# Delta rule and routed experts: batch 1 of expert 0 gets dates of its own in the planner

## The chip, the cores and the metric

The kernel runs on one core of one Trainium2 chip. The metric is the device time of one execution in microseconds. The engines are TensorE (PE; its weight loads are shown apart as PEld), VectorE (DVE), ScalarE (ACT), GpSimd (POOL) and SyncE (SP, which here only issues transfers). The granted clock of PE is given as a share of full speed.

## The reference

The first half is a delta rule over 4 batches x 8 heads, 768 steps, head size 48; its outputs, regrouped, are the 3072 tokens (384 wide) of a router that sends each token to two of eight experts, each two matrices with a ReLU between.

```python
k_n = k / (np.linalg.norm(k, axis=-1, keepdims=True) + 1e-06)
for t in range(S):
    y[:, :, t] = np.einsum('bhd,bhde->bhe', q[:, :, t], state)
    v_old = np.einsum('bhde,bhd->bhe', state, kt)
    state = state + bt[:, :, :, None] * np.einsum('bhd,bhe->bhde', kt, vt - v_old)
...
logits = x @ w_gate
noise_scale = np.log1p(np.exp(x @ w_noise))
noisy_logits = logits + noise_scale * noise
top2 = np.argpartition(-noisy_logits, 2, axis=1)[:, :2]
...
h = np.maximum(x[mask] @ w1[e], 0.0)
out[mask] += top2_w[mask, k, None] * (h @ w2[e])
```

## The kernel before

**The delta rule in chunks.** The 768 steps are 12 chunks of 64. A unit is one chunk of two batches, so there are 24 units, n = 0 to 23, in two independent state streams; four units (two chunks) make a step s = 0 to 5. For each step one triangular matrix per head and chunk is inverted on DVE, column by column (`invert`, lines 743 and 747; the results `tb` and `tt` are written at lines 770 and 778), after which PE joins blocks (`join`, lines 821 and 827). A unit then goes through `within` (the product of queries and keys, masked on DVE into qk, line 864), `recur` (state times keys on PE, line 612; the difference from v on DVE, line 914; state times queries, "of_state", line 885; "solve", line 930; the new state, gathered on PE at line 952 and added on DVE at line 964) and `answer` ("of_chunk", line 989; the store of the rows of y, line 395; the turn of y, line 999; the router product with `wgn`, line 1004, whose result ACT copies to the logits, line 1035). The turns of k and q are at line 594. `v` is multiplied by norms on POOL (line 894).

**Routing.** `route` handles steps 0 and 1, steps 2 and 3, step 4 and step 5, in four turns: ACT and DVE find the two experts and their weights, PE counts earlier tokens of each expert (`count_earlier`, lines 1126 to 1132), DVE makes row numbers, and POOL scatters one list entry per token and choice into `tokens_x` in DRAM by indirect transfers ("spreads", line 437). `cut` caps a count.

**Early tiles.** Expert 0's first five tiles of 128 tokens are worked on as soon as the list holds enough: batch 1 (tiles 0 and 1) after step 1's routing, batch 2 (tiles 2 and 3) after step 3, batch 3 (tile 4) after step 4. For a batch, `early` loads its list (`load_meta`, SP, line 1268), gathers token rows (POOL, line 401), turns them (PE, line 1294; copied by ACT, line 1302), multiplies them in eight groups by `w1` (PE, line 1313; ReLU on ACT, line 1324), back by `w2` (PE, line 1337, in four pieces a tile), scales by the gate (DVE, line 1349), and, for batch 1 alone, adds them to `out` by an indirect transfer at once (`put_early`, POOL, line 456).

**The planner.** None of this is emitted in program order. Every piece above is a job with an engine, an estimated cost, readers and writers, PSUM banks and an optional due time. `Jobs.order` plays the jobs through in time by those estimates and fixes one order for every engine. Among jobs that could start at the same moment it takes the one with the smallest key. Due times are handed back from a job to those before it. Each engine then executes its jobs in exactly that order, whatever the real times are; an instruction that waits holds up everything behind it on its engine. Early jobs carry `late`, which sorts them behind all other jobs:

```python
job.key = (0, job.due) if job.late is None else (1, job.late)
```

**After the rule** (`rest`, and a loop over experts 1 to 7, written out by hand): SP loads the lists of all experts once the last spreads have landed (line 421), POOL gathers the rest of expert 0 and expert 1's rows `xr` (line 401), SP regroups `xr` into `xq` (line 1562), DVE turns that into `xe` (line 1572) and makes sums of its blocks (line 1514). PE finishes the rest of expert 0 (lines 1686 to 1712) and starts expert 1 with the products of the sums (line 1548). Experts 1 to 7 follow each other with PE as the busiest engine. `t_w`, `s_w`, `s_x` are sums of weight and token blocks.

Of the kernel before, what the change touches and what calls it, by code (L numbers as in the profile page):

```python
# [25 lines left out]
EARLY_BANK = 2, (0, 1, 2)  # L26
EARLY = {1: [(0, 2)], 3: [(2, 4)], 4: [(4, 5)]}
EARLY_TILES = 5
PUT_IN_RULE = 1
ROWS = TILES * 128 + MORE  # L30
META = 3
# [65 lines left out]
class Jobs:  # L97
# [13 lines left out]
        self.wrote, self.read = {}, {}  # L111

    def add(self, engine, cost, emit, reads=(), writes=(), opens=None, uses=None, closes=None,
            lands=0.0, moves=0.0, due=None, late=None, apart=0.0):
        job = SimpleNamespace(
            engine=engine, cost=cost * (self.SLOW if engine == self.PE else 1.0), emit=emit, opens=opens, closes=closes, lands=lands,
            moves=moves,
            due=1e9 if due is None else due, late=late, apart=apart, after=set(),
            number=len(self.jobs),
        )  # L120
        bank = opens or uses or closes
        if bank:

            if bank.users:
                job.after.add(bank.users[0])
            if closes:
                job.after.update(bank.users)
            if uses and engine == self.PE:
                job.after.update(bank.users)
            bank.users.append(job.number)  # L130
        for key in reads:
            job.after.update(self.wrote.get(key, ()))
        for key in writes:
            job.after.update(self.wrote.get(key, ()))
            job.after.update(self.read.get(key, ()))
        for key in reads:
            self.read.setdefault(key, []).append(job.number)
        for key in writes:
            self.wrote[key], self.read[key] = [job.number], []
        job.after.discard(job.number)  # L140
        self.jobs.append(job)

    def order(self):
        jobs = self.jobs
        for job in reversed(jobs):
            for i in job.after:
                jobs[i].due = min(jobs[i].due, job.due - job.cost - self.SIGNAL)
        for job in jobs:
            job.key = (0, job.due) if job.late is None else (1, job.late)
        waits = [len(job.after) for job in jobs]  # L150
        then = [[] for _ in jobs]
        for job in jobs:
            for i in job.after:
                then[i].append(job.number)
        ready = [0.0] * len(jobs)
        could = [set() for _ in self.ENGINES]
        for job in jobs:
            if not job.after:
                could[job.engine].add(job.number)
        free = [0.0] * len(self.ENGINES)  # L160
        empty = {size: [0.0] * len(x) for size, x in self.banks.items()}
        spaced = moved = 0.0

        def place(size, among):

            return min(
                ((empty[size][i], i) for i in among if empty[size][i] is not None),
                default=None,
            )

        done = []
        while len(done) < len(jobs):
            first = {}
            best = None
            for engine in self.ENGINES:
                at = []
                for i in could[engine]:
                    start = max(free[engine], ready[i], spaced if jobs[i].apart else 0.0)
                    if jobs[i].opens:
                        which = jobs[i].opens.size, jobs[i].opens.among  # L180
                        if which not in first:
                            first[which] = place(*which)
                        room = first[which]
                        if room is None:
                            continue
                        start = max(start, room[0])
                    at.append((start, jobs[i].key, i))
                if at:
                    soon = min(at)[0] + self.PATIENCE
                    pick = min((x for x in at if x[0] <= soon), key=lambda x: x[1:])  # L190
                    best = min(best or (1e9,), pick)
            start, _, i = best
            job = jobs[i]
            could[job.engine].remove(i)
            end = free[job.engine] = start + job.cost
            if job.apart:
                spaced = start + job.apart
            if job.opens:
                size, among = job.opens.size, job.opens.among
                job.opens.at = x = first[size, among][1]  # L200
                empty[size][x] = None
                job.opens.tile = self.banks[size][x]
                for y in job.opens.users:
                    if jobs[y].late is None:
                        jobs[y].key = 0, min(jobs[y].due, end + self.SOON)
            if job.closes:
                empty[job.closes.size][job.closes.at] = end + self.SIGNAL
            job.start = start
            if job.moves:
                end = moved = max(moved, end) + job.moves  # L210
            done.append(job)
            for j in then[i]:
                ready[j] = max(
                    ready[j],
                    end + (self.SIGNAL + job.lands if jobs[j].engine != job.engine else 0.0),
                )
                waits[j] -= 1
                if not waits[j]:
                    could[jobs[j].engine].add(j)
        return sorted(done, key=lambda job: job.start)  # L220
# [13 lines left out]
def kernel(  # L234
# [52 lines left out]
    FT = F // 128  # L287
# [178 lines left out]
    def deltanet(ictx):  # L466
# [4 lines left out]
        jobs = Jobs(  # L471
            [psum.tile([128, 512], FP32, name=f"single{i}") for i in range(2)],
            [psum.tile([128, 2, 512], FP32, name=f"pair{i}") for i in range(3)],
        )
        PE, ACT, DVE, POOL, SP = Jobs.ENGINES
# [771 lines left out]
        early_xe = sb([128, KT, 256], "early_xe")  # L1247
        early_hT = sb([128, FT, 256], "early_hT")
# [7 lines left out]
        def early(s, lo, hi):  # L1256
# [2 lines left out]


            n, rows = hi - lo, (hi - lo) * 128
            w1e, w2e = held["w"]
            of_steps = [
                ("rows", x, i, y) for x in range(s + 1) for i in range(US) for y in (0, 1)
# [2 lines left out]
            def load_meta():  # L1267
# [7 lines left out]

            jobs.add(
                SP, 0.7, load_meta, reads=of_steps, writes=[("early_meta", lo)], lands=2.0,
                moves=0.3, late=lo,
            )
            units = (s + 1) * US  # L1280
            for i in range(n):
                at = lo + i
                x, x_key = early_x[at % 4], ("early_x", at % 4)
                jobs.add(
                    POOL, 1.2,
                    lambda x=x, at=at: [take_rows(x, place_of(early_meta[:, at]), units)],
                    reads=[("early_meta", lo), *(("stored", i) for i in range(units))],
                    writes=[x_key], lands=2.0, moves=0.7, late=lo,
                )
                p = early_bank()  # L1290

                def turned_rows(x=x, p=p):
                    for do in range(KT):
                        nc.tensor.transpose(
                            flat(p)[:, do * 128 : (do + 1) * 128],
                            chunk(x, do), ident,
                        )

                jobs.add(PE, 0.5, turned_rows, reads=[x_key], opens=p, late=lo)
                jobs.add(  # L1300
                    ACT, 0.5,
                    lambda i=i, p=p: nc.scalar.copy(
                        early_xe[:, :, i * 128 : (i + 1) * 128],
                        flat(p)[:, 0 : KT * 128].rearrange("p (k t) -> p k t", t=128),
                    ),
                    writes=[("early_xe", i)], closes=p, late=lo,
                )
            for fo in range(FT):
                p = early_bank()

                def inner_of(fo=fo, p=p):
# [5 lines left out]

                jobs.add(
                    PE, 0.0038 * rows, inner_of, reads=[("early_xe", i) for i in range(n)] + ["w1"],
                    late=lo + 0.1, opens=p,  # L1320
                )
                jobs.add(
                    ACT, 0.12 + rows * 0.0011,
                    lambda fo=fo, p=p: nc.scalar.activation(
                        early_hT[:, fo, 0:rows], flat(p)[:, 0:rows], ACTF.Relu
                    ),
                    writes=[("early_hT", fo)], closes=p, late=lo + 0.1,
                )
            for i in range(n):
                at = lo + i  # L1330
# [2 lines left out]
                for f0 in range(0, FT, 2):  # L1333

                    def back(i=i, p=p, f0=f0):
# [4 lines left out]
                            )  # L1340

                    jobs.add(
                        PE, 0.98, back, late=lo + 0.2,
                        reads=[("early_hT", f0), ("early_hT", f0 + 1), "w2"],
                        **({"uses": p} if f0 else {"opens": p}),
                    )
# [3 lines left out]
                        got, flat(p)[:, 0:DM], early_meta[:, at, 1:2]  # L1350
                    ),
                    reads=[("early_meta", lo)], writes=[got_key], closes=p, late=lo + 0.2,
                )
                if s > PUT_IN_RULE:
                    held["puts"].append(lambda got=got, at=at: put_early(got, at))
# [525 lines left out]
```

## Time and profile before

| | |
|---|---|
| median of 3 runs | 817.26 us (814.52 to 818.99) |
| profiled execution | 819.58 us, of which the span from first to last instruction is 817.8 us |
| granted PE clock, mean of the span | 0.897 |
| busy PE, DVE, POOL, ACT | 727.6, 566.7, 414.3, 311.6 us |
| last router product of the rule ends | 325.3 us |
| expert 1 begins on PE | 395.5 us |

PE is busy 89% of the span, but the span has stages with different limits. Expert 1 and what follows take about half of it. The other half is the delta rule, and between the two stands a stretch in which PE works on early tiles and the rest of expert 0 while POOL, SP and DVE bring up expert 1's tokens. Where a row of the timeline has brackets, they give the idle time of the engine just before the row and what ended it.

### The profile page before, as it was taken

What the parts mean: (1) busy time and instruction counts of PE and PEld (TensorE: products, weight loads), DVE (VectorE), ACT (ScalarE), POOL (GpSimd) and SP (SyncE); (2) the same over time, 40 slices, a digit from 0 to 9 for tenths busy, and PEclk for the clock granted to TensorE, in tenths of its full rate; (3) what the DMA queues carried; (4) which work ended last, traced back from release to release, by engine and by line L of the source; (5) the groups of instructions that cost most, each with busy time, mean ns of one, the idle gap of its engine ahead of it and who ended that gap; (6) DMA issues with size and microseconds to landing.
All of it is one profiled execution on the core that took longest, in us unless ns stands there. A gap on an engine that the chain in (4) does not pass through costs nothing.

```text
span 817.8 us, 22648 instructions
## 1 busy us (share of the span) xinstructions
PE 727.6 (89%) x9365; PEld 572.8 (70%) x9365; DVE 566.7 (69%) x1256; ACT 311.6 (38%) x740; POOL 414.3 (51%) x398
## 2 busy tenths in 40 slices
PE   4665887887889889999999999999999999999993
PEld 3445776676778779778568678578587597596693
DVE  4899889998899631303588487587686785785841
ACT  3547394846764542112250430430521511502500
POOL 2102100105520633569677786886886886787032
PEclk9955789768868656999999999999999999999998
DMA  2465636633333102464645444553445346333031
GB/s 47 78 111 126 184 96 157 175 73 67 61 72 71 43 23 40 156 105 84 183 112 120 126 132 83 146 154 56 144 142 104 100 138 129 89 59 43 0 38 26
DMA packets 142928, 79.61 MB, mean 97 GB/s; under 512 B 118624, under 2 KB 139232, under 8 KB 141792
## 3 DMA queue, kind: packets, MB, share of 16 engines
q1 hardware_dynamic: 128096, 57.94, 27.1%
q0 software_dynamic: 12544, 19.75, 13.7%
q8 instruction: 75, 1.23, 0.7%
q10 hardware_dynamic: 2176, 0.39, 0.3%
q14 instruction: 37, 0.30, 0.2%
HBM read 49.85 MB, written 20.03 MB: 85 GB/s over the span
## 4 chain that ended last, share of the span: by engine, by line
PE 60%; DVE 21%; issue 10%; POOL 3%; SPq 2%; ACT 1%; DMA 0%; DVEq 0%; POOLq 0%; ACTq 0%
PE inner L1548 25%; PE outer L1548 14%; DVE part L743 6%; DVE t L747 5%; PE pair L1313 3%; PE pair L1337 3%; PE pair L612 2%; POOL out_dram L456 2%; PE inner L1659 2%; PE single L1004 1%; SPq L546 1%; DVE t L662 1%; DVE qk L864 1%; PE pair L989 1%; SPq L562 1%
## 5 line engine op out<-in xcount | busy, mean ns | idle before, releaser
L1615 ACT ACTIVATE hT<-inner 128x416 f32<-128x416 f32 x112 | 57.9, 517 | 260.8 <-PE inner L1548 259.4
L1609 DVE TENSOR_TENSOR hT<-hT,inner 128x416 f32<-128x416 f32 x182 | 105.6, 587 | 64.0 <-PE inner L1548 55.9
L456 POOL DMA_INDIRECT out_dram<-sums,metas_x x51 | 83.6, 1639 | 94.4 <-DVE sums L1448 67.1
L437 POOL DMA_INDIRECT tokens_x<-meta,slot x48 | 48.7, 1014 | 97.8 <-DVE t L756 33.0
L1548 PE MATMUL inner<-s_x,w1e 128*128 128x416 f32 x196 | 78.7, 512 | 0.0
L743 DVE TENSOR_TENSOR part<-t 128x30 f32<-128x30 f32 (+9 forms) x180 | 69.2, 384 | 4.7
L747 DVE TENSOR_TENSOR t<-t,part 128x30 f32<-128x30 f32 (+9 forms) x180 | 64.3, 357 | 6.2
L1604 ACT ACTIVATE hT<-hT 128x416 f32<-128x416 f32 x112 | 59.9, 547 | 12.1 <-DVE hT L1609 6.8
L401 POOL DMA_INDIRECT xr<-rows_y,metas_x x49 | 56.4, 1152 | 14.0 <-issue 13.0
L712 POOL TENSOR_SCALAR_AFFINE_SELECT t<-t 128x1024 f32<-128x1024 f32 x6 | 7.6, 1268 | 107.5 <-DVE ss L683 107.5
L1548 PEld LDWEIGHTS inner<-s_x,w1e 128*128 128x128 f32 x196 | 37.2, 190 | 31.2 <-issue 29.0
L1548 PE MATMUL inner<-xe,w1e 128*128 128x416 f32 x140 | 58.1, 513 | 0.0
L1548 PE MATMUL outer<-t_w,hT 128*128 128x192 f32 x336 | 58.0, 326 | 0.0
L1548 PE MATMUL inner<-s_x,s_w 128*128 128x416 f32 x140 | 56.9, 512 | 0.0
L1548 PEld LDWEIGHTS outer<-t_w,hT 128*128 128x128 f32 x336 | 55.2, 190 | 0.0
L1514 POOL TENSOR_TENSOR w1e<-w1e 128x256 f32<-128x256 f32 x63 | 53.5, 858 | 2.3
L1548 PE MATMUL outer<-w2e,hT 128*128 128x192 f32 x280 | 50.7, 328 | 0.3
L1548 PEld LDWEIGHTS outer<-w2e,hT 128*128 128x128 f32 x280 | 46.1, 190 | 4.3 <-issue 2.2
L894 POOL TENSOR_TENSOR v<-v,norms 128x384 f32<-128x384 f32 x24 | 22.8, 967 | 46.3 <-DVE norms L726 25.5
L1548 PEld LDWEIGHTS inner<-s_x,s_w 128*128 128x128 f32 x140 | 26.6, 190 | 22.3 <-issue 22.3
L1548 PEld LDWEIGHTS inner<-xe,w1e 128*128 128x128 f32 x140 | 26.4, 190 | 20.7 <-issue 16.2
L801 ACT COPY w<-tt 32x256 f32<-32x256 f32 x96 | 38.6, 402 | 5.5 <-DVE tt L778 3.5
(191 smaller groups left out, 1594.1 us busy)
## 6 DMA issues: line engine op xcount, KB each, us to landing
w1e<-in_moe_w_dram SPq DMA_DIRECT2D x8, 1536.0 KB
w2e<-in_moe_w_dram SPq DMA_DIRECT2D x8, 1536.0 KB
xq<-xr SPq DMA_DIRECT2D x56, 84.0 KB
qp<-in_q_dram SPq DMA_DIRECT2D x48, 96.0 KB
v<-in_v_dram SPq DMA_DIRECT2D x48, 96.0 KB
out_dram<-empty SPq DMA_DIRECT2D x4, 1152.0 KB
rows_y<-y SPq DMA_DIRECT2D x24, 192.0 KB
kp<-in_k_dram SPq DMA_DIRECT2D x88, 48.0 KB
```

The lines of the kernel that those rows point to most:

```text
L401: d = nc.gpsimd.indirect_dma_start(out=got, out_offset=None, in_=rows_y[0 : units * 128], in_offset=bass.IndirectOffsetOnAxis(ap=index, ax ...
L437: d = nc.gpsimd.indirect_dma_start(out=tokens_x, out_offset=bass.IndirectOffsetOnAxis(ap=slot, axis=0), in_=meta, in_offset=None, bounds_c ...
L456: d = nc.gpsimd.indirect_dma_start(out=out, out_offset=bass.IndirectOffsetOnAxis(ap=index, axis=0), in_=got, in_offset=None, bounds_check= ...
L743: v_.tensor_tensor(out=part, in0=t[:, :, j + 1 :, j, None].to_broadcast(shape), in1=t[:, :, None, j, 0:j].to_broadcast(shape), op=ALU.mult,)
L747: columns[:] = [v_.tensor_tensor(out=t[:, :, j + 1 :, 0:j], in0=t[:, :, j + 1 :, 0:j], in1=part, op=ALU.add).ins]
L801: lambda rows=rows, cols=cols, w64=w64, tt=tt: nc.scalar.copy(w64[rows, :, cols], tt[rows]),
L1313: nc.tensor.matmul(flat(p)[:, 0:rows], w1e[:, do, fo * 128 : (fo + 1) * 128], early_xe[:, do, 0:rows], start=(do == 0), stop=(do == KT - 1),)
L1514: engine.tensor_tensor(out=block(to), in0=block(x), in1=block(y), op=ALU.add if sign == "+" else ALU.subtract,)
L1548: nc.tensor.matmul(p, lhsT, rhs, start=opens and i == 0, stop=i == len(products) - 1, skip_group_check=True,)
L1604: nc.scalar.activation(h, h, ACTF.Relu)
L1609: nc.vector.tensor_tensor(out=h, in0=h, in1=p, op=ALU.add if sign > 0 else ALU.subtract)
L1615: nc.scalar.mul(h, p, float(sign))
```

## The change

A table `WITHIN` gives batch 1 (the batch that follows step 1) a beginning and a pace in the planner's time: its i-th piece may not be placed before 215 + 3 i and is due one unit later. Piece 0 is the loading of the list, the gathers and the turns; pieces 1 to 8 are the eight inner groups with their ReLUs; then follow the eight pieces of the products back and the two gatings. Jobs get a `begin`, and a job with a due time is now sorted by it even if it has `late`; the other jobs of the rule without a due time are sorted as before, ahead of later batches. The due times of batch 1 are also handed back to what it reads. Batches 2 and 3, and the puts of batch 1, keep `late` alone.

```diff
+WITHIN = {1: (215.0, 3.0)}
...
-            due=1e9 if due is None else due, late=late, apart=apart, after=set(),
+            due=1e9 if due is None else due, late=late, apart=apart, after=set(), begin=begin,
...
-            job.key = (0, job.due) if job.late is None else (1, job.late)
+            job.key = (0, job.due) if job.due < 1e8 else (1, job.late or 0.0)
...
-        ready = [0.0] * len(jobs)
+        ready = [job.begin for job in jobs]
...
+            begin, pace = WITHIN.get(s, (None, 0.0))
+
+            def at_step(i):
+                if begin is None:
+                    return {}
+                at = begin + i * pace
+                return {"due": at + 1.0, "begin": at}
...
-                moves=0.3, late=lo,
+                moves=0.3, late=lo, **at_step(0),
...
-                    writes=[x_key], lands=2.0, moves=0.7, late=lo,
+                    writes=[x_key], lands=2.0, moves=0.7, late=lo, **at_step(0),
...
-                jobs.add(PE, 0.5, turned_rows, reads=[x_key], opens=p, late=lo)
+                jobs.add(
+                    PE, 0.5, turned_rows, reads=[x_key], opens=p, late=lo, **at_step(0)
+                )
...
-                    late=lo + 0.1, opens=p,
+                    late=lo + 0.1, opens=p, **at_step(1 + fo),
...
-                        PE, 0.98, back, late=lo + 0.2,
+                        PE, 0.98, back, late=lo + 0.2, **at_step(1 + FT + i * FT // 2 + f0 // 2),
...
+                    **at_step(1 + FT + (i + 1) * FT // 2),
```

On PE, the new order puts the first two turns and the inner groups of batch 1 among the pieces of units 16 and 17, and the last product back ahead of the second state product of units 18 and 19. The pieces of the rule that stood there follow later. On SP the loading of batch 1's list moves behind six other transfers and the store of unit 14; on POOL its gathers move behind four products of v and norms.

More of the change, by code (lines that the diff above doesn't have):

```diff
@@ L113, in add @@
     def add(self, engine, cost, emit, reads=(), writes=(), opens=None, uses=None, closes=None,
-            lands=0.0, moves=0.0, due=None, late=None, apart=0.0):
+            lands=0.0, moves=0.0, due=None, late=None, apart=0.0, begin=0.0):
         job = SimpleNamespace(
@@ L1305, in early @@
                     ),
-                    writes=[("early_xe", i)], closes=p, late=lo,
+                    writes=[("early_xe", i)], closes=p, late=lo, **at_step(0),
                 )
@@ L1326, in early @@
                     ),
-                    writes=[("early_hT", fo)], closes=p, late=lo + 0.1,
+                    writes=[("early_hT", fo)], closes=p, late=lo + 0.1, **at_step(1 + fo),
                 )
```

## The prediction

> **What bounds the kernel now.** I read the granted clock first (0.897 over the span), then the busy time by stage, then the chain of work that ended last, then engine timelines along one data path. The stage table (busy time of PE, PEld, DVE, ACT, POOL, each with its count; then clock, DMA share, GB/s):
>
> ```profile
> 245.00:275.00 30.00, 25.39 (x836) 22.21 (x836) 27.99 (x88) 12.69 (x30) 3.41 (x3) 0.90 0.33 76
> 275.00:295.00 20.00, 17.70 (x558) 15.84 (x552) 8.32 (x28) 14.44 (x39) 16.52 (x18) 0.59 0.08 13
> 295.00:320.00 25.00, 23.37 (x472) 21.76 (x473) 5.51 (x20) 6.17 (x16) 2.62 (x6) 0.50 0.09 28
> 320.00:345.00 25.00, 24.39 (x106) 18.39 (x105) 7.16 (x35) 5.20 (x16) 13.97 (x15) 0.97 0.49 143
> 345.00:395.00 50.00, 48.31 (x233) 36.62 (x233) 13.12 (x26) 9.18 (x27) 36.09 (x39) 1.00 0.57 113
> ```
>
> Up to 275 the last inversion fills DVE and PE has holes; from 275 the delta rule is PE's, at half clock, nearly without holes. From 320 PE runs early batches. The chain of waits in that stretch (start, us, what):
>
> ```profile
> 322.14 2.59 PE pair L1313 x12
> 324.74 0.57 PE single L1004 x6
> 325.31 6.57 PE pair L1313 x30
> ...
> 344.61 10.63 PE pair L1313 x48
> 355.24 10.32 PE pair L1337 x32
> ...
> 392.84 2.73 PE outer L1712 x16
> 395.57 0.55 PE inner L1548
> ```
>
> L1004 ending at 325.31 is the rule's last router product: the last PE piece of the recurrence. From there PE has 70 us of early tiles and leftovers until expert 1 starts (L1548, 395.5). It looks as if PE alone set that date. The timelines of the other engines show a second path that is nearly as long:
>
> ```profile
> 325.35 0.17 ACT L1035 COPY logits<-single 128x16 f32<-128x16 f32 x1 [0.19 <-PE single L1004]
> 346.16 0.98 POOL L437 DMA_INDIRECT tokens_x<-meta,slot  x1 [0.30 <-DMA tokens_x<-meta,slot]
> 351.63 5.79 SPq L421 DMA_DIRECT2D metas_x<-tokens_x  x8
> 354.07 1.07 POOL L401 DMA_INDIRECT early_x<-rows_y,early_meta  x1 [3.14 <-DMA metas_x<-tokens_x]
> 365.96 0.95 POOL L401 DMA_INDIRECT xr<-rows_y,metas_x  x1 [0.30 <-issue]
> 369.23 10.47 SPq L1562 DMA_DIRECT2D xq<-xr  x16
> 381.25 3.98 DVE L1572 STREAM_TRANSPOSE xe<-xq 128x384 f32<-128x384 f32 x7 [2.82 <-DMA xq<-xr]
> 390.54 1.08 DVE L1514 TENSOR_TENSOR s_x<-s_x,xe 128x416 f32<-128x416 f32 x2
> ```
>
> Last logits, routing on DVE, eight spreads on POOL (last issue 346.16), token lists (351.63), gathers (to 366.9), regrouping, turns, sums: done at 391.6. So the rule's last product plus 66.3 us gives expert 1 its operands, 3.9 us before PE arrives. Expert 1 onward is dense PE work at clock 1.00, unchanged by the edit.
>
> **What the Trainium skill says.** "TensorE: Matmul & The Clock Gate", Part 1 on the HAM clock gate: the clock is halved by default, an idle window of about 3.4 us halves it again, a busy one of that length restores it, with nothing between. The trace agrees on two levels (1.00 and 0.50), but not on "busy": in 300 to 320 PE shows no hole and stays at 0.50, and holes of 1.55 us (before 274.06) and 2.91 us sufficed to lose the clock. "Runtime: NRT & Kernel Launch", Instruction fetch mechanics: instructions are streamed in blocks of 256, mostly hidden. The trace has unexplained stops that may be this:
>
> ```profile
> 245.08 1.11 PE L885 MATMUL pair<-st,qT 64*64 64x48 f32 x32 [2.26 <-DVE qk L864]
> 274.06 1.07 PE L821 MATMUL single<-tb,at 32*32 32x32 f32 x32 [1.55 <-DVE missing L1226]
> 296.54 0.53 PE L827 MATMUL single<-w,x 32*32 32x32 f32 x11 [2.91 <-issue]
> ```
>
> "DMA: Bandwidth & Descriptors", Anatomy of one DMA: about 2 us fixed. Here a gather into early_x takes 4.5 us from issue to landing, and early_meta 2.6 us (227.41 to 230.03); I use those.
>
> **The change, part by part.** No instruction is added or removed: the 1,469 jobs stay and are reordered on all five queues.
>
> *Moved out of the tail.* Batch 1: eight inner groups spaced 1.295 us (ACT's early_hT rows, L1324), 10.4; sixteen products back 10.3 (the row at 355.24); six transposes 1.0: 21.7 us of PE at full clock.
>
> *Moved into the rule.* In the new order the first transpose stands where PE waits at 245.08, ahead of of_state of unit 16. SP issues the list load after the two v loads, two q loads and the store of unit 14 (ready at 234.5) instead of at 227.41: about 235.1, landing 237.7. On POOL the four v-times-norm products go first (last ends 237.98), the gathers go at 238.0 and 239.3 and land at 242.5 and 243.9. PE is free at 242.8, so the transposes use the 2.26 us hole. This is the only large hole they meet. A cover of a microsecond at most: if the gathers come 3 us late, PE and all behind it stand 3 us.
>
> *PE up to the end of batch 1*, at full clock: 21.7 of batch 1; fifteen groups of the rule at 0.66 (four turns or 32 matmuls, such as L930 and L952 near 254), 9.9; two joins 1.6; two turns of y 1.1; two router products 1.7; a count and a cut 2.4: 38.4. From 243.3 that is 281.7, and 285.2 with the start at half clock until about 252. Checked for waits: DVE reaches qk of unit 17 at 263, after seven mid columns (0.87 each), the routing (4.0) and seven more (5.3), and PE asks for it at 269; tb is ready by 270 and no longer waited for. The gather of states of unit 16 falls from 251.2 to about 274: nothing of the recurrence advances meanwhile.
>
> *PE from there to the last router product*: 35 groups at 0.66, 23.1; joins 3.4; six turns of y 3.3; six router products 5.0; count and cut 2.0; two early transposes and one inner group of batch 2, 2.4: 39.2. So 324.4 at full clock without a hole, almost the old 325.3: the moved 21.7 us are paid by the half-clock time and holes that the old order had there.
>
> *What I expect of those.* Issue stops between 245 and 325 were 0.34, 0.42, 0.51 and 2.91, 4.2 in all; the joins that hold them are all still there, so I keep 4.2. Half clock took 44 us of 275 to 321; one group costs 1.05 us then against 0.66, so a microsecond loses 0.38. With the waits on DVE gone I take a third, 15 us, losing 5.7 (none: 0; all: 17). The rule then ends at 334.3, 9.0 later.
>
> *Where the stall goes.* Routing, lists, gathers, regrouping follow the rule's end, so they come 9.0 later; each is an own SP or POOL issue and none is removed. PE's work after the rule's end falls to about 52 us (70.2, less the 17.0 of batch 1 behind 325.3, less 1.3 for an inner group of batch 2 done by then), so PE is early and waits. Of the 66.3 us I take off 1.0, as the two products that open expert 1 don't need the last sum, and 1.0, as batch 3's gather (354.07, 1.07 plus 0.37) now goes before the last spreads: bounds 0 and 1.4. Expert 1's operands: 334.3 + 64.3 = 398.6. PE has then stood about 12 us and restarts at half clock: 1.7 (half of 3.4; 0 to 3.4). So 400.3 against 395.5 in effect: **+4.8 us**. The profiled execution (819.58, span 817.8) becomes about 824.4; on the median of 817.26, **822.0**.
>
> ACT's ten copies and ReLUs (4.0 us) and DVE's two gatings (1.2) only change place: ACT is busy 12.7 of 30. The list load on SP has only the store of unit 15 behind it. The two puts on POOL (1.6 each) wait for the gatings and hold up the spreads of the second routing, 1.29 apart: about 4 us, for which only batch 2's list waits, and PE doesn't want that before 320; bare, it would cost those 4 us.
>
> **Rivals.**
> 1. *The clock stays up*, as dense 128-row products stand among small ones and the waits on DVE vanish. The rule ends at 321 to 327, expert 1 begins 2.5 to 8.5 us sooner (end + 64.3 + 1.7 against 395.5): 809 to 815. For it: half clock at 275 and 244 followed waits that go. Against it: no early piece stands after the last product back until batch 2, some 35 us of small groups. It decides where the rule's end is less than 4.2 us late; below zero late it gives faster by over 0.5%.
> 2. *PE remains the bound after the rule*: then the 18 us of PE work gone from behind 325.3 would show, but the data path takes over after 3.9 us: 813. Against it: only 3.9 us of slack exist.
> 3. *Half clock all through, or the recurrence starved*: the rule ends 16 to 20 late: 829 to 834. For it: in 295 to 320 half clock never ended by itself.
> 4. *Nothing happens*: gains and losses inside 4 us, 814 to 821.
>
> **How the numbers follow.** About 0.5% (4.1 us) is what a measurement can tell from no change here. The forecast (rule 7 to 14 late, 819.5 to 827.5): 0.45; rival 1 with 2: 0.22, two thirds of it below 813.2 (0.15, and 0.01 for rival 4's lower end); rival 4 as a case of its own: 0.20; rival 3: 0.13. Slower by over 0.5%: 0.34 of the forecast's share and rival 3's 0.13, 0.47; faster 0.16; the rest 0.37. With a tenth left out at each end, in rivals 1 and 3: 811 to 829.5.
>
> **What would show it.** Right: L1004's last product later than 329, clock of 0.5 somewhere between 290 and its end; PE idle before the first L1548 with DVE's s_x or the xq transfer as releaser; everything after shifted by one constant. L1294 first near 243. Wrong: PE without a wait before L1548, the last L1004 before 325, or a wait for early_x over 2 us.

## The result, and the profile after

The changed kernel takes 821.27 us, the kernel before 815.82 us in the same comparison: ratio 1.0068, 95% interval 1.0040 to 1.0096, or 5.5 us more (two disturbed executions of the changed kernel are left out of the ratio). The forecast was 822.0.

The two profiled executions do not show these 5.5 us as such: that of before (819.58) lies 3.8 us above its median, that of after (817.91 us, span 816.2) 3.4 us below. They show two parts of opposite sign, and their sum is 1.6 us less; no profile shows the 5.5 us of this chip at work, so their make-up is inferred from the parts and from runs on other chips:

| us | before | after |
|---|---|---|
| last router product of the rule ends | 325.3 | 331.0 |
| expert 1's first two products (they do not need the last sum) start | 395.5 | 387.2 |
| the first product that needs the last sum starts | 397.0 | 393.66 |
| from the rule's end to that product | 71.7 | 62.7 |
| from there to the end of the span | 420.8 | 422.5 |
| stops of PE from 240 to the rule's end: waits for DVE and ACT | 7.19 | 3.87 |
| stops there that the profile calls "issue" | 4.18 | 8.98 |
| half clock from 240 to the rule's end | 51.2 | 10.2 |

(The last row adds up the clock intervals of the trace.) The stage table of the kernel after has the columns of the one shown of before: stretch and length, then busy time and count of PE, PEld, DVE, ACT and POOL, then clock, DMA share and GB/s.

```profile
245.00:275.00 30.00, 30.00 (x485) 23.98 (x486) 26.42 (x80) 13.47 (x33) 3.34 (x4) 0.90 0.22 48
275.00:295.00 20.00, 16.24 (x469) 12.60 (x470) 4.18 (x10) 10.47 (x28) 15.60 (x16) 1.00 0.27 41
295.00:320.00 25.00, 19.78 (x778) 17.48 (x770) 9.65 (x32) 9.92 (x28) 5.93 (x8) 0.93 0.23 52
320.00:345.00 25.00, 24.49 (x308) 20.78 (x308) 9.20 (x49) 8.33 (x24) 10.84 (x11) 1.00 0.39 136
345.00:395.00 50.00, 39.34 (x183) 27.44 (x182) 13.84 (x28) 7.36 (x22) 35.26 (x41) 0.93 0.56 141
```

Before, 275 to 320 ran at clock 0.59 and 0.50 with PE 41 of 45 us busy; now the clock is 0.93 to 1.00 and PE is busy for 36 of 45. The clock came back and holes came with it. From 345 to 395 PE is idle for 10.7 us, before for 1.7. PE's timeline shows the first turns of batch 1 behind the old hole of 2.26 us, which they did not fill (PE still waits for DVE's qk), and then three of the new stops:

```profile
244.82 0.91 PE L1303 MATMUL pair<-ident,early_x 128*128 128x128 f32 x3 [2.26 <-DVE qk L865]
289.14 0.18 PE L822 MATMUL single<-tb,at 32*32 32x32 f32 x1 [1.60 <-issue]
293.29 0.68 PE L931 MATMUL pair<-v,w 64*64 64x48 f32 x31 [2.16 <-issue]
302.21 0.80 PE L613 MATMUL pair<-qT,kT 64*64 64x64 f32 x20 [1.22 <-issue]
```

Behind the rule the chain of waits, which before stayed on PE all the way to expert 1, now leaves PE at 371.7:

```profile
330.42 0.57 PE single L1005 x6
330.99 9.16 PE pair L1324 x42
...
370.72 0.99 PE outer L1709 x6
371.71 0.23 SPq L1574
...
381.10 2.09 DMA xq<-xr
...
383.27 3.86 DVE xe L1584 x7
...
392.43 1.10 DVE s_x L1526 x2
393.53 0.14 issue
393.66 2.41 PE inner L1560 x4
```

The regrouping transfers, DVE's turns and the sums set expert 1's start, and PE waits for DVE's sums:

```profile
349.30 0.98 POOL L438 DMA_INDIRECT tokens_x<-meta,slot  x1 [0.30 <-issue]
351.87 0.98 POOL L438 DMA_INDIRECT tokens_x<-meta,slot  x1 [0.30 <-issue]
355.16 4.75 SPq L422 DMA_DIRECT2D metas_x<-tokens_x  x8
371.25 10.45 SPq L1574 DMA_DIRECT2D xq<-xr  x16
387.22 3.11 PE L1560 MATMUL inner<-xe,w1e 128*128 128x416 f32 x4 [5.68 <-issue]
393.66 1.03 PE L1560 MATMUL inner<-s_x,s_w 128*128 128x416 f32 x2 [3.33 <-DVE s_x L1526]
```

### The profile page after: what moved, and what is told of

Same layout as the page of the kernel before. It is cut to its first block, busy times and chain, and to the rows that moved or that the text cites. A ratio compares the mean times of both kernels' runs of the same rounds, so it can differ in the third digit from the quotient of the medians.

```text
span 816.2 us, 22647 instructions
## 1 busy us (share of the span) xinstructions
PE 711.9 (87%) x9365; PEld 554.7 (68%) x9365; DVE 567.6 (70%) x1256; ACT 311.3 (38%) x740; POOL 412.4 (51%) x398
## 4 chain that ended last, share of the span: by engine, by line
PE 63%; DVE 15%; issue 10%; SPq 3%; ACT 3%; POOL 3%; DMA 1%; DVEq 0%; POOLq 0%; ACTq 0%
PE inner L1560 25%; PE outer L1560 14%; DVE part L744 4%; PE pair L1324 3%; PE pair L1348 3%; DVE t L748 3%; PE pair L613 3%; POOL out_dram L457 2%; PE single L595 2%; PE pair L990 2%; PE pair L931 2%; PE inner L1671 2%; SPq L547 1%; PE pair L886 1%; DVE s_x L1526 1%
## 5 line engine op out<-in xcount | busy, mean ns | idle before, releaser
L1560 PE MATMUL inner<-xe,w1e 128*128 128x416 f32 x140 | 60.3, 530 | 5.7 <-issue 5.7
L1584 DVE STREAM_TRANSPOSE xe<-xq 128x384 f32<-128x384 f32 (+1 forms) x49 | 29.7, 645 | 18.9 <-DMA xq<-xr 18.9
```

The source lines that it names most:

```text
L1560: nc.tensor.matmul(p, lhsT, rhs, start=opens and i == 0, stop=i == len(products) - 1, skip_group_check=True,)
L1584: return lambda: nc.vector.transpose(out=out, in_=in_)
```

## The experiments

Two questions were open: does the data path really set expert 1's start now, and what makes the rule end later. The theory is the prediction's: PE work moved into the rule delays it, half clock and stops included, and the data path carries the delay to expert 1. The rivals: PE still sets the start (2), and a rule made late by its order rather than by the amount of work (3, "recurrence starved").

The runs fell on several chips, each group beside runs of the kernel before on its own chip: 831.2 us for the first four runs, 830.6 for the next four, 814.6 for the next three, 829.6 for the last. All ratios are to that.

### The kernel after once more

> The changed kernel once more, for a second profile. Theory A (the rule ends later and the path routing, lists, gathers, regrouping, turns, sums carries that to expert 1): expert 1 begins 62 to 64 us after the last router product in this profile too, whatever the clock was; time against before +4 to +7 us. Theory B (the loss is made of stalls inside the rule that vary, and PE sets expert 1's start): the distance differs by several us between profiles.

Measured: 851.81 us, ratio 1.0251 (1.0202 to 1.0300). The same kernel loses 20.6 us on this chip and 5.5 on the first. Instruction by instruction it is 32.4 to 33.1 us behind the profile of after from 339 us of that profile on to the last product; 30.4 of these are there when the rule ends, at 361.4. Expert 1's first product that needs the last sum follows 64.6 us after that (62.7 in the first profile; 62 to 64 expected), so the path behind the rule nearly keeps its length. The 4 to 7 us more than before that were expected were missed by far. Within the rule are 50.6 us of half clock after 240 and 16.0 us of issue stops, most of them of a kind that is rare in the first profile:

```profile
346.19 0.47 PE L931 MATMUL pair<-v,w 64*64 64x48 f32 x5 [0.47 <-issue]
347.62 0.46 PE L931 MATMUL pair<-v,w 64*64 64x48 f32 x4 [0.96 <-issue]
349.04 0.48 PE L931 MATMUL pair<-v,w 64*64 64x48 f32 x4 [0.95 <-issue]
350.47 0.47 PE L931 MATMUL pair<-v,w 64*64 64x48 f32 x4 [0.95 <-issue]
```

One group of 32 products, 0.66 us elsewhere, comes out four products at a time, each 1.43 us apart, here at half clock (0.72 in other places). From 240 to the rule's end, gaps of 0.45 to 1.6 us between two products of one group hold 18.8 us here, 4.6 in the profile of after, 1.8 in that of before. On the three chips where the kernel before takes about 830 us its rule has them too (4.7 to 14.9 us), and it is some 15 us slower there than on the first chip. The rule itself suffers most on those chips: that of the kernel after ends at 358.7 to 369.0 us in the four profiles that leave it unchanged, that of the kernel before at 328.1, 333.9 and 334.5 in three.

### Behind the rule: nine additions more on DVE

```diff
             for turn in turns():
                 turn()
+            for _ in range(9):
+                nc.vector.tensor_tensor(
+                    out=s_h[0][:, 0], in0=empty, in1=empty, op=ALU.add
+                )
             add_up(nc.vector, SUMS_X, xb)
```

In the kernel after:

> Adds nine additions of 128 x 384 on DVE (about 5 us by the rows of that size) between the turns and the sums of expert 1's tokens, in the changed kernel. Theory A: this path sets expert 1's start: +4.5 to +5.5 us on the changed kernel, so +9 to +12 on before. Theory B: the path has slack: under +2 on the changed kernel.

In the kernel before:

> Adds nine VectorE additions of 128x384 (about 0.57 us each, 5.1 us) to the kernel before, between the turns of expert 1's rows and their sums, as was done to the kernel after (which lost 3.8 us by it). If in the kernel before PE's own work sets when expert 1 starts and the data path has 3.9 us of room, at most 1.2 us is lost: ratio 1.000 to 1.002, and the first real product of expert 1 follows VectorE's last sum at once. If the data path set that start before as well, all 5.1 us is lost: 1.006.

Measured: after 855.65 us, ratio 1.0316 (1.0268 to 1.0363), 3.8 us more than the same kernel without them on that chip (4.5 to 5.5 expected, and each interval is 4 us to either side, so the profile has to decide); before 832.15, ratio 1.0023 (1.0002 to 1.0045), 1.9 us more (at most 1.2 expected, inside the interval). First the wait ahead of expert 1 in the kernel after with the additions, then the two rows that matter in the kernel before with them:

```profile
428.58 1.72 PE L1560 MATMUL inner<-s_x,s_w 128*128 128x416 f32 x2 [8.40 <-DVE s_x L1526]
```

```profile
402.81 1.66 PE L1548 MATMUL inner<-xe,w1e 128*128 128x416 f32 x4
403.04 1.09 DVE L1514 TENSOR_TENSOR s_x<-s_x,xe 128x416 f32<-128x416 f32 x2
```

In the kernel after PE waits 8.40 instead of 3.32 us: all 5.1 us arrive. In the kernel before PE comes to expert 1 without a hole, and DVE, made 5.3 us later by the additions, ends at 404.1, just ahead of the first product that needs the sum (404.3). So before the start was PE's; the room of the data path is 5.4 us when it is counted to that product (391.6 to 397.0 in the profile of before), not the 3.9 that the prediction counted to the first product of all. After, the start is the data path's. Rival 2 falls.

### Behind the rule: gathers exchanged, regrouping shared with ACT

```diff
+            load_rows(1)
             for i, size in enumerate(rows_in[t0:]):
                 take_rows(rest_x[0:size, i], place_of(metas_x[0:size, 0, t0 + i]), NT)
-            load_rows(1)
-            regroup()
+            regroup(nc.sync, range(0, 2))      # range(0, 4) where only the gathers are exchanged
...
+            regroup(nc.scalar, range(2, 4))    # behind the ReLUs of the rest (kernel after)
```

> The kernel after, with the gathers of expert 1's rows on POOL ahead of the gathers of the rest of expert 0. If the data path from the rule's end to expert 1 sets the end, it is shorter by two gather issues, about 2.6 us: span down 2 to 3 us, ratio to the kernel before lower by 0.003 than that of the kernel after on the same chip (1.025 there). If PE's work behind the rule sets it, nothing is won, or 1 to 2 us is lost as the rest of expert 0 gets its rows later.

> As the run with the two gathers exchanged in the kernel after, and half of the sixteen regrouping transfers of expert 1's rows are issued by ACT after its ReLUs of the rest, instead of all by SP. SP took 10.5 us for sixteen. If the data path sets the start of expert 1: 2.6 us by the exchange and about 5 by the halved issue, 7 to 8 us less than the kernel after: ratio near 1.016 where the kernel after has 1.025. If PE's work behind the rule sets it: within 1 us of the kernel after. If ACT's ReLUs come late, the second half comes late with them and only the 2.6 us are won.

> The same two edits in the kernel before: gathers exchanged, the regrouping transfers shared between SP and ACT (here ACT's half right behind SP's in the program). If PE's own work sets the start of expert 1 in the kernel before: no change, 0.998 to 1.002. If the data path set it there too: 5 to 8 us less, 0.990 to 0.994.

Measured: exchanged gathers in the kernel after 848.02 us, ratio 1.0214 (1.0162 to 1.0265); with ACT's half besides 871.95, ratio 1.0488 (1.0433 to 1.0543); both edits in the kernel before 832.05, ratio 1.0017 (0.9995 to 1.0039). The exchange alone is 0.0037 better than the kernel after had been, but on another chip and inside the intervals: not settled. In its profile the last sum ends 64.0 us after the rule, against 64.5 in the run of the kernel after: 0.5 of the 2.6 us that were expected. The shared version in the kernel after missed by far. Its rows of SP, ACT, DVE and PE:

```profile
409.85 4.96 SPq L1574 DMA_DIRECT2D xq<-xr  x8
423.09 0.33 ACT L1713 ACTIVATE hT<-inner 128x192 f32<-128x192 f32 x1 [0.65 <-PE inner L1709]
423.33 9.65 ACTq L1574 DMA_DIRECT2D xq<-xr  x8
440.02 3.83 DVE L1584 STREAM_TRANSPOSE xe<-xq 128x384 f32<-128x384 f32 x7 [35.79 <-DMA xq<-xr]
443.96 2.42 PE L1560 MATMUL inner<-xe,w1e 128*128 128x416 f32 x3 [13.01 <-issue]
```

The exchange delays the rest's rows (ACT's last ReLU ends 54.6 us after the rule with the exchange alone, 45.1 without it), so here that ReLU ends at 423.4, and ACT's eight transfers go out at 1.2 us each: the turns start at 440.0, in the run with the exchange alone at 419.4. Of these 20.6 us 3.2 come from the rule's end; the kernel lost 23.9. I had foreseen that ACT could be late, not that it would cost more than the exchange gains. The miss says the same as the additions: what is late on this path is late at the end. In the kernel before nothing was won, as PE sets the start, and the shared issue wasn't quicker either (eight transfers in 11.74 us on SP while ACT issued the other eight).

### The rule: most of batch 1's products left out

```diff
-                    for do in range(KT):
+                    last = 1 if lo == 0 else KT
+                    for do in range(last):
...
+                        if lo == 0 and f0:
+                            return
-                        for fo in (f0, f0 + 1):
+                        for fo in (0,) if lo == 0 else (f0, f0 + 1):
```

Two thirds of batch 1's inner products and fourteen of sixteen products back are left out, in the kernel after and in the kernel before; the order of everything else stays. About 5.8 us of batch 1 are left.

> Leaves out two of three matmuls of each inner group of batch 1 and 14 of its 16 products back (about 6.9 + 9.0 = 15.9 us of PE), so tiles 0 and 1 of expert 0 come out wrong. Theory A: that work stands ahead of the rule's end, and expert 1 waits for that end: 10 to 16 us faster than the changed kernel, so 5 to 11 us faster than before. Theory B: PE is held by waits and not by the work, so at most 5 us faster than the changed kernel.

> The same matmuls left out of the kernel before, where they stand behind the rule. Theory A: PE gets to expert 1 15.9 us earlier and then waits for the operands: only 3 to 5 us faster than before, minus up to 2 for the half clock after the pause. If PE alone set expert 1's start before the change: 14 to 16 us faster.

Measured: after 849.16, ratio 1.0239 (1.0180 to 1.0297); before 827.44, ratio 0.9971 (0.9948 to 0.9994). In the kernel after the theory missed, and theory B (at most 5 us faster) came true: 15.9 us of PE work less in the rule, and its end moved from 361.4 to 360.9. The kernel before without these products is 2.4 us faster by the ratio and 3.8 by the medians, near what its theory A expects (3 to 5, minus up to 2) and far from the 14 to 16 that would follow if PE alone set expert 1's start. The stage tables, of the kernel after without these products and then of the kernel before without them:

```profile
245.00:275.00 30.00, 25.22 (x526) 21.02 (x526) 27.66 (x86) 14.99 (x39) 1.02 (x2) 0.76 0.27 61
275.00:295.00 20.00, 11.76 (x202) 9.49 (x203) 6.66 (x15) 7.63 (x20) 12.92 (x13) 0.50 0.12 13
295.00:320.00 25.00, 20.53 (x665) 17.84 (x659) 4.34 (x10) 9.93 (x26) 11.69 (x14) 0.70 0.26 48
```

```profile
245.00:275.00 30.00, 26.94 (x822) 23.54 (x825) 27.90 (x87) 15.84 (x40) 0.00 (x0) 0.81 0.23 50
275.00:295.00 20.00, 15.45 (x381) 12.84 (x378) 8.36 (x19) 9.33 (x25) 15.27 (x16) 0.63 0.20 43
```

Same program work, same chip, other order: the rule ends at 360.9 in the new order, with most of the 5.8 us of batch 1 ahead of that end, and at 328.1 in the old one. From 240 on the new order has 81.9 us of half clock against 41.0, and 18.1 us of waits for DVE and ACT against 5.8. So the order alone can cost as much as the whole change does on this chip. That the recurrence is put off is the likely reason, but no run separates it from the other effects of the order. With the left-out products in their place there are 50.6 us of half clock and 2.4 us of those waits: they had kept the clock up for longer and covered the waits.

### The rule: the same amount of PE work without the order

Sixteen bursts of products that nothing reads, in the kernel before, ahead of the pieces of the rule that open a bank:

```diff
+            if job.engine == self.PE and job.opens and job.start > 224.0 and loads < 16:
+                self.load(job.opens, loads)
+                loads += 1
             job.emit()
...
+            times, cols = (KT, 256) if k < FT else (2, DM)
+            for i in range(times):
+                nc.tensor.matmul(
+                    into[:, 0:cols], ident, empty[:, 0:cols],
+                    start=(i == 0), stop=(i == times - 1),
+                )
```

> The kernel before, its order kept, with extra PE work of batch 1's size and shape that nothing reads: from the place where PE waits at 245 us on, sixteen bursts of 128-row products with a constant (eight of three products of 256 columns, eight of two of 384, about 20.7 us at full clock), each ahead of one piece of the rule that opens a bank. If it is the amount of PE work moved into the rule that makes it end later, the rule ends 10 to 20 us later than in the kernel before (328 to 334 us on the chip of the last runs) and so does the kernel: ratio 1.012 to 1.025. If it is the new order, in which the recurrence is put off behind batch 1, the extra work goes into holes and buys back the clock: the rule ends 0 to 8 us later, ratio at most 1.010, with less of the rule at half clock than the 37 to 51 us of the kernel before.

Measured: 831.31 us, ratio 1.0213 (1.0167 to 1.0259). The rule ends at 335.0, 9.7 later than in the profile of before: in this pair 20.7 us of added work cost half of their length. The other half was paid by stops (11.4 us from 240 to the rule's end before, 5.3 now) and half clock (51.2 before, 33.2 now). But the profile of before lies 3.8 us above its median, and this one 2.0 below: by the medians the kernel loses 16.7 us, four fifths of the added work. Behind the rule PE has all its old work, and expert 1 starts 70.2 us after the rule's end, as before, so the loss lies in the rule as far as these profiles show. The amount of work delays the rule as well, then: the end time expected for "amount" (10 to 20 later) is all but met and its ratio is met, that for "order" (at most 1.010) isn't. Both causes exist. How they share the loss on one chip was not measured: the order alone ran on one chip, the amount alone on another.

### The rule: other dates for batch 1

```diff
-WITHIN = {1: (215.0, 3.0)}
+WITHIN = {1: (260.0, 3.0)}     # the other run: (215.0, 0.0)
```

> The kernel after with batch 1 planned from 260 instead of 215, three apart as before: the recurrence up to there keeps the order of the kernel before, and batch 1's products come among the last chunks. If the order (the recurrence put off from 251 to 274 us) makes the rule late, it ends at least 10 us sooner than in the kernel after (361 us on the chip of the last runs): ratio near 1.012. If the amount of PE work does it, or the supply of instructions to PE, nothing changes by more than 3 us: ratio 1.020 to 1.028.

> The kernel after with all pieces of batch 1 wanted at 215 at once instead of three apart. The recurrence is put off by the same work in one piece. If putting it off makes the rule late, the rule ends 0 to 6 us later than in the kernel after: ratio 1.023 to 1.033. If it is the alternation of dense and small products (changes of clock, supply of instructions), fewer alternations make it sooner by 5 us or more: ratio under 1.019.

Measured: from 260 on 833.95 us, ratio 1.0245 (1.0204 to 1.0285); all at once 828.46, ratio 1.0151 (1.0104 to 1.0198). The expectations took the kernel after at 1.025; on this chip, where before took 814.6, the first chip's 1.0068 is the likelier measure, and neither number decides as it was meant to. Both are slower than that. With the later date the rule ends at 344.6, of which 7.4 us are one wait on PE that the later place makes, for rows of batch 2 ahead of the last router product:

```profile
340.09 0.91 PE L1303 MATMUL pair<-ident,early_x 128*128 128x128 f32 x3 [7.42 <-DMA early_x<-rows_y,early_meta]
```

All at once, the rule ends at 339.7 with 30.7 us of half clock from 240 on; spread, it was 331.0 and 10.2 on the first chip. As far as two chips can be compared, spreading helps; no run of the kernel after on this chip confirms it.

### Stops and clock by themselves

Behind the end of the kernel before, with constant operands and no other engine involved:

```diff
+        pause(1)                       # one addition on DVE writes the operand
+        for i in range(32):            # 128x384 products: the clock comes up
+            nc.tensor.matmul(outer[0][:, 0:DM], ident, rhs, start=(i == 0), stop=(i == 31))
+        small(48)                      # 48 x 32 calls, 64x48, two products each in the trace
+        pause(16)
+        small(48)
```

> The kernel before with three stretches of PE work that nothing reads behind its end, to measure the stops and the clock without the recurrence: 32 products of 128x384 to bring the clock up, then at once 48 groups of 32 products of 64x48 (the shape of the delta rule's groups, constant operands, no wait on another engine), then a pause of about 9 us in which VectorE writes their operand sixteen times, and the same 48 groups again. A group took 0.66 us at full clock and 1.05 at half in the rule. If only the clock and the PE's own speed set the rule's pace, the first stretch keeps the clock at 1.00 and takes 31 to 34 us without stops. If PE is also limited by the arrival of its instructions, in transfers of 16 KB that came 3.4 to 3.9 us apart at the shortest in the rule (256 instructions of 64 bytes, 128 products with their weight loads), the first stretch takes 41 to 47 us, with a stop of about 1 us for most of its twelve transfers, each ended 1.2 to 1.6 us after the transfer. For the second stretch: if a PE that is busy without a hole gets its clock back, it falls to the pace of the first within about 10 us; if not, it runs at half clock to its end, 50 us.

A call of this form is two products in the trace, so each stretch has 3,072 products and 24 transfers of instructions, twice what the expectation counts: 82 to 94 us with a limit from the instructions, 62 to 68 without. Measured: 85.9 us for the first stretch, which the limit from the instructions explains. Some of PE's rows, then the traffic from 841 to 856 us (forty slices of 0.375 us), in which nothing but instructions moves:

```profile
842.50 2.08 PE L1818 MATMUL inner<-s_h,ident 64*64 64x48 f32 x128 [0.98 <-issue]
846.24 2.08 PE L1818 MATMUL inner<-s_h,ident 64*64 64x48 f32 x128 [1.67 <-issue]
...
864.15 3.03 PE L1818 MATMUL inner<-s_h,ident 64*64 64x48 f32 x128 [1.94 <-issue]
868.16 5.82 PE L1818 MATMUL inner<-s_h,ident 64*64 64x48 f32 x256 [0.99 <-issue]
```

```profile
GB/s 0 0 0 0 0 0 44 0 0 0 0 0 0 0 0 0 0 44 0 0 0 0 0 0 0 0 44 0 0 0 0 0 0 0 0 44 0 0 0 0
q8 instruction: 4, 0.07, 1.7%
```

At full clock PE runs exactly 128 products (256 instructions with their weight loads) in 2.08 us and then stands, mostly for 1.4 to 1.7. In the window of the traffic a transfer of 16 KB starts about 1.1 us after PE has begun a block (at 843.6 and 847.4 for the first two rows), takes 0.9 to 1.1, and PE goes on 1.2 to 1.5 us after its end: 3.5 us a block at best, 3.6 on average over the 47.8 us below. At 865.0 the clock fell to half for 6.8 us, in the midst of the stream, and the next 256 products, two blocks, went through without a stop between them. In the second stretch, before the clock came back, 228 products took 6.05 us at half clock without a stop, 3.4 us per 128. For a stream of such products the full clock gains nothing. In the table below each row is a stretch at one clock:

```profile
864.96:871.78 6.82, 5.83 (x216) 5.56 (x208) 0.00 (x0) 0.00 (x0) 0.00 (x0) 0.50 0.02 5
940.00:987.80 47.80, 27.24 (x1686) 25.63 (x1683) 0.00 (x0) 0.00 (x0) 0.00 (x0) 1.00 0.02 4
933.90:940.00 6.10, 6.05 (x228) 6.05 (x231) 0.00 (x0) 0.00 (x0) 0.00 (x0) 0.50 0.02 5
```

Applied to the rule: in the profile of after all eight issue stops end 1.2 to 1.6 us after the end of a transfer on this queue (that of 293.29 after one from 290.9 to 291.9), and from 304 to 326 the transfers start 3.4 to 4.1 us apart, the pace of the stretch above. In the profile of before it holds for all four, 4.18 us. In the isolated stretch no other engine and no other transfer is at work, so those stops come from the arrival of instructions; in the rule the same timing says so. The gaps of 0.72 and 1.43 us on the three slower chips do not follow the transfers in this way; what makes them stays open.

## Why the prediction was right, and where by luck

**What bounds the kernel.** PE set the date of expert 1, and the data path was ready a few microseconds earlier: confirmed by the additions on DVE in both kernels. The room was 3.9 us to the first product and 5.4 to the first that needs the last sum.

**Moved into the rule.** The gathers were issued at 238.4 and 239.8 (238.0 and 239.3 foreseen). But the turns did not use the 2.26 us hole: their rows were there by 243.0, and the first turn ran at 244.8, as late as the product that stood in its place before. What it waited for was DVE's qk, which presumably freed its bank in PSUM. The prediction checked the rows and not the bank.

**PE up to the end of batch 1.** The last product back ends at 284.0 (285.2 foreseen, from a start 1.5 us earlier). The wait for the inverse is gone, as said.

**PE from there to the last router product.** 39.2 us foreseen; the 47.0 us to 331.0 less 9.0 of issue stops, 0.2 of other waits and 1.3 lost to half clock are 36.5.

**What I expect of those.** Here both terms were mis-sized, in opposite directions. "I keep 4.2" for issue stops: 9.0. The reason given, that joins hold the stops, fails too: only two of the eight stand ahead of a join (lines 822 and 828), the others wherever a block of instructions ran out. "I take a third, 15 us, losing 5.7" for half clock: 3.4 us after batch 1, losing 1.3. The step that failed is to treat them as independent, as the isolated stretch suggests. At half clock the instructions arrive about as fast as PE uses them up (3.5 us a block against 3.4 in the stretch); once the clock is up, PE outruns them and stands. In a long row, the small groups that I priced at 0.66 us at full clock would follow each other no faster than every 0.87 us, by an estimate from the stretch (32 of 128 products in 3.5 us), against 1.05 at half clock in the rule. The rule's end came 5.7 us later in the profile (9.0 foreseen): 3.3 better, 3.9 of it from the two work terms and -0.6 from these. That these errors nearly cancelled is luck.

**Where the stall goes.** Right in kind. The last sum ended 62.5 us after the rule, not 66.3: 1.4 went with batch 3's gather (1.0 taken), 2.2 between the last spread and the loading of the lists (5.5 us before, 3.3 after; before, the two puts of batch 1 stood there, at 347.5 and 349.4, which I had priced only at their new place; that they made the difference isn't shown), 0.2 elsewhere. The two opening products ran at 387.2, inside the wait, and so took 1.5 us off PE's work behind the last sum (1.0 taken). The restart at half clock cost what was foreseen: the first product behind the last sum comes 3.3 us sooner than before, those from 398.2 on 1.6 us sooner, so 1.8 us (1.7 taken) went there.

**The sum.** From the profiled execution it gave +4.8; the pair of profiles shows -1.6, as the rule's end and the path behind it (62.7 us for 64.3 plus 1.7) each came out 3.3 us better, and the medians show +5.5. The profile of after lies 3.4 us below its median and that of before 3.8 above, 7.2 us together; I expected the profiled execution to be as typical after as before. So 822.0 beside 821.3 is nearer than its parts deserve. On the chips where before took about 830 us the step "the rule ends 9 later" would have been short by 15 us at the least: there the rule ends at 328.1 to 334.5 before and at 358.7 to 369.0 after.

**Rivals.** Rival 1's premise came true, a clock that stays up; it didn't gain, since stops for instructions took its place. Rival 3 comes nearest to what the slower chips show: 44 to 72 us of half clock from 240 to the rule's end in the four profiles of the rule after, and 20.6 us lost. The prediction's reading of the Trainium skill ("Runtime: NRT & Kernel Launch", Instruction fetch mechanics: blocks of 256 instructions, the crossing mostly hidden) kept the block and doubted the hiding; the isolated stretch at full clock shows mostly 1.4 to 1.7 us per block not hidden. Its reading of the clock, that holes of 1.55 and 2.91 us "sufficed" to lose it, does not hold: the clock fell at 294.4, 0.8 us into the second hole, which began at 293.6, and in the isolated stretch it stood at 1.00 for 47.8 us with a stop of up to 1.9 us in every block.

## What to carry to other kernels

Before you price a stage at full clock, count its instructions: where many small products stand in a row, the arrival of their blocks can be the pace, and the clock then buys little. Moving work into a stage that has holes can cost half of its length (by the pair of profiles here) to four fifths (by the medians) even if the holes are real; and a hole is only of use to work whose every condition, its buffer too, is met in time. Compare the cost with what the move frees behind the stage until the next path takes over (here 5.4 us, and 3.8 more as that path became shorter). And test a forecast on two profiles, and two chips: one execution may lie 3.8 us from the median, and another chip may answer 20 us instead of 5.

## What was not expected of the hardware

- PE's instructions come in transfers of 16 KB, 256 instructions; in a stream of 64x48 products at full clock, 2.08 us of work is followed by 1.4 to 1.9 us of stop, 3.5 us a block at best.
- A PE at half clock got its full clock back after 6.1 us of a dense stream (228 products), though in the kernel before 295 to 320 stayed at 0.50 with PE 23.37 of 25 us busy. So "busy" in this profile is not what brings the clock back, and "Part 1" of the page "TensorE: Matmul & The Clock Gate" of the Trainium skill (a busy window of about 3.4 us restores the clock) agrees with the stream, not with the word busy as the profile uses it. What does count stays open: those 25 us held 472 products, half the rate of the stream, but 45 of them were of larger shapes and took about half of the time.
- With 1.4 to 1.9 us of stop in each 3.5 to 4 us the clock stayed at 1.00 for 47.8 us, twice. It then fell to 0.50 while the stream went on, four times in all (at 865.0, 919.6, 987.8 and 1011.7), and came back after 3.4 to 10.2 us. What tips it isn't shown.
- On three of the chips PE at times took four to six products per 0.72 us, or four per 1.43 us at half clock, inside one group. No run tells why.
